# State tables of a convolution kernel: waves by chunk or by pairs of chunks

## The chip, the cores and the metric

The kernel runs on one core of one Trainium2 chip. The metric is the device time of one execution in microseconds (us), as a median over runs. The engines are TensorE (PE; its weight loads are PEld), VectorE (DVE), ScalarE (ACT), GpSimd (POOL) and SyncE (SP), which issues most DMAs. Each engine has its own in-order queue of instructions.

## The reference

The input u is 2048 x 512. After a layer norm over channels, two branches are computed and joined:

```
xn = layernorm(u)
K[d, l] = Re sum_n C[d,n] * dt[d] * B[d,n] * exp(dt[d] * A[d,n] * l)     # 512 channels, 128 states, 2048 steps
s = causal_convolution(xn, K) + xn * Dskip                               # by FFT in the reference
h = gelu(layernorm(xn) @ w1); shifted by -+1, -+2 steps per quarter of the channels; x1 = xn + hs @ w2
g = silu(x1 + gelu(layernorm(x1) @ w3) @ w4)                              # the MLP is 512 -> 1376 -> 512
out = u + s * g
```

A, B and C are complex. The kernel K of the convolution is a sum over 128 states of a decaying exponential times a wave, for each channel and step.

## The kernel before, in words

**The work.** The convolution goes through spectra: `u_stage1` and `u_spectra` transform the input, `kstage1` and `products(hf)` transform K and multiply, `inverse` and `finish` go back and add. The token mixing (`token_mixing`, with `h_pair` and `hs_pair`) and the MLP (`mlp`, eight groups of 256 steps) make the gate. The MLP runs in f16 pairs: `ph` by 12 matmuls of 256 columns, a gelu on ScalarE into `g`, two halves `ghl`, then 6 matmuls of 512 columns into `pa`.

**The state tables.** `tables(hf)` (lines 1060 to 1069) makes K for one half of the channels, in eight chunks of 32 channels (16 chunks in all, `CQ = 32`). It splits a step l into 64 fine positions and 32 coarse ones, so that K is a matrix product of a fine and a coarse table over the states. For a chunk `cc`:

- `phases` (line 989): two VectorE products of 128 x 1024 make the phases of the fine and the coarse table in `pt`; a shift by a large constant into `kt` rounds them to whole turns. The shift (`E.shift`) may run on ScalarE or VectorE.
- `remainders` (line 1011): one VectorE instruction of 128 x 2048 leaves the part of a turn.
- `waves` (line 1015): the absolute value into `kt` (`E.abs`, either engine), the sine of `pt` and the sine of `kt` plus a quarter turn (the cosine), both 128 x 2048 on ScalarE.
- `factors` and `sums` (lines 1021 and 1031): six VectorE products with the exponentials `mag`, `ea`, `eb`; then 256 small matmuls on TensorE, a copy `kev` and a DMA to HBM.

`block` (line 947), once for four chunks, makes those exponentials on ScalarE; `angle` (line 929), once for two chunks, small products. The pair `kt`, `pt` of a chunk lies in one of two buffers (`phpair`, line 779), taken in turn. In the trace all tiles of these two buffers have the name `pt`.

**Activation tables.** ScalarE holds one table set at a time. `TABLES` (line 104) gives the sets: exponentials are set 1, sine and silu set 2, gelu set 3. Before an operation of another set than the current one a table load is put in (line 512).

**The order of the work.** No engine's order is written by hand. All operations are recorded in a `Plan` (line 310) as objects with costs, and what they depend on is found from the places that they read and write. `order` (line 426) then runs through time: whenever an engine is free, it takes among its ready operations the one with the smallest due time, out of the list `DUE` (line 127, 1733 numbers, one for each operation in the order of recording), corrected by a few penalties: `SWITCH = 54.15` (line 258) where ScalarE would have to load another table, `KEEP` where TensorE would change its array mode, and `PREFER`, `AVOID`, `PREFERP`, `AVOIDP` where an operation may run on either of two engines:

```
if e == "ACT" and o.table and o.table != table:
    v += SWITCH
```

`together` (line 416) joins everything recorded inside it to one operation, which the planner places as one piece. It is used for the exponentials of a block and for groups of matmuls. While TensorE waits for longer, `issue` (line 506) fills its idle time with products of an identity.

Every instruction is issued in one of two lines, so the profile names line 515 for nearly all of them; 512 is the table load and 514 the filling products. The tiles tell them apart.

Of the kernel before, what the change touches and what calls it, by code (L numbers as in the profile page):

```python
# [27 lines left out]
TWO_PI = 6.283185  # L28
# [64 lines left out]
class Op:  # L93
# [163 lines left out]
)  # L257
SWITCH = 54.15
PREFERP, AVOIDP = 37.15, -7.22
PREFER, AVOID = -2.21, 23.48  # L260

# [404 lines left out]
def kernel(  # L666
# [393 lines left out]
    def tables(hf):  # L1060
        for cc in range(8 * hf, 8 * hf + 8):
            if cc * CQ % BQ == 0:
                block(cc * CQ // BQ)
# [464 lines left out]
```

## Time and profile before

| | |
|---|---|
| median of 3 runs | 564.96 us (564.07 to 565.45) |
| the profiled execution's own time | 567.52 us |
| its span, first to last instruction | 565.7 us |
| granted TensorE clock, mean | 0.986 |
| table loads on ScalarE | 49 of 1283 ns |

In a row of a group stand the engine, the operation, output and input tiles with partitions x elements, the count, then busy time, mean ns of one instruction, the idle time of the engine just before the group, and what ended it. In a row in order of time stand start, duration, engine, line and operation, in brackets an idle time before it and its releaser. Times in a row of windows are busy times inside that stretch.

### The profile page before, as it was taken

Reading aid. Unit: us, or ns where it says so; the run is one execution under the profiler, and the core shown is the slowest. Engines: PE = TensorE matmul, PEld = TensorE weight load, DVE = VectorE, ACT = ScalarE, POOL = GpSimd, SP = SyncE. Lnnn points to the kernel's source line nnn. Section 1 sums busy time; section 2 is a strip of 40 time slices with the busy share of each in tenths; the row PEclk is TensorE's granted clock in tenths of the full one; section 3 lists DMA queues with packets and bytes.
Section 4 is the critical chain, followed back from the end, with each engine's and each line's share of the span. In section 5 each row is a group of like instructions: output and inputs, shape, how many; then the busy total and the mean of one; then the engine's idle time right before and its main releaser. Section 6 shows DMA issues by size and latency. Waiting matters only on the chain.

```text
span 565.7 us, 14303 instructions
## 1 busy us (share of the span) xinstructions
PE 534.8 (95%) x6114; PEld 351.5 (62%) x6114; DVE 462.5 (82%) x706; ACT 411.6 (73%) x592; POOL 0.7 (0%) x6
## 2 busy tenths in 40 slices
PE   9979999999887899999999999999999999999982
PEld 8966776874443456567667666676665667567530
DVE  4999998999999989999999999999245257453566
ACT  2999997999968989978999997994436353232420
POOL 0000000000000000000000000000000000000000
PEclk9999999999999899999999999999999999999995
DMA  9996758345755224754224324326758558839977
GB/s 198 228 213 223 239 204 284 112 134 150 264 183 188 93 76 87 224 187 123 77 103 140 103 85 134 123 66 207 249 226 281 202 189 281 273 134 234 314 226 233
DMA packets 69695, 103.14 MB, mean 182 GB/s; under 512 B 14784, under 2 KB 48832, under 8 KB 68736
## 3 DMA queue, kind: packets, MB, share of 16 engines
q1 hardware_dynamic: 68864, 100.13, 57.5%
q10 hardware_dynamic: 768, 2.10, 1.1%
q8 instruction: 48, 0.79, 0.6%
q14 instruction: 15, 0.12, 0.1%
HBM read 64.46 MB, written 37.75 MB: 181 GB/s over the span
## 4 chain that ended last, share of the span: by engine, by line
PE 60%; DVE 20%; ACT 8%; DMA 7%; issue 3%; SPq 0%; DVEq 0%
PE pb L515 23%; PE pa L515 18%; DVE pt L515 11%; PE pc L515 10%; PE pd L515 9%; DVE X L515 4%; DMA X<-in_A_u_dram 4%; ACT pt L515 2%; ACT mag L515 2%; DVE pr L515 2%; ACT L512 1%; DMA rawA<-in_A_A_re_dram 1%; DMA cst<-c_gp 1%; DMA rawC<-in_A_C_im_dram 1%; DVE ghl L515 1%
## 5 line engine op out<-in xcount | busy, mean ns | idle before, releaser
L515 PE MATMUL pb<-x1T,w3h 128*128 128x256 f16 (+1 forms) x1056 | 123.2, 273 | 0.2 <-ACT g L515 0.2
L515 PE MATMUL pa<-w4h,ghl 128*128 128x512 f16 (+1 forms) x528 | 121.9, 379 | 0.0
L515 PEld LDWEIGHTS <-w3h 128*128 128x128 f16 (+1 forms) x1056 | 102.9, 100 | 23.7 <-issue 8.2
L515 PEld LDWEIGHTS <-ghl 128*128 128x128 f16 (+1 forms) x528 | 49.6, 98 | 61.7 <-issue 8.5
L512 ACT ACT_TABLE_LOAD x49 | 62.9, 1283 | 7.4 <-issue 5.9
L515 PE MATMUL pd<-w,hT 128*128 128x512 f32 x116 | 55.1, 617 | 6.4 <-DVE X L515 5.0
L515 PE MATMUL pb<-xT,w 128*128 128x256 f32 x256 | 59.4, 383 | 1.3 <-ACT xT L515 1.3
L515 DVE TENSOR_TENSOR pt<-mag,pt 128x1024 f32<-128x1024 f32 x48 | 57.6, 1215 | 0.7 <-ACT pt L515 0.7
L515 PEld LDWEIGHTS pb<-xT,w 128*128 128x128 f32 x256 | 47.2, 190 | 12.8 <-issue 3.2
L515 ACT ACTIVATE pt<-pt 128x2048 f32<-128x2048 f32 x28 | 53.3, 1907 | 0.3 <-DVE pt L515 0.2
L515 ACT ACTIVATE g<-pb,wsc 128x512 f32<-128x512 f32 (+1 forms) x48 | 30.8, 649 | 30.7 <-PE pb L515 28.6
L515 DVE SCALAR_TENSOR_TENSOR ghl<-g,wsc,ghl 128x512 f16<-128x512 f32 (+1 forms) x48 | 33.3, 700 | 22.4 <-ACT ghl L515 22.3
L515 ACT ACTIVATE ghl<-g,wsc 128x512 f16<-128x512 f32 (+1 forms) x37 | 24.7, 680 | 28.7 <-PE pa L515 28.5
L515 PEld LDWEIGHTS pd<-w,hT 128*128 128x128 f32 x116 | 21.9, 196 | 33.0 <-issue 25.9
L515 ACT ACTIVATE mag<-par 128x128 f32<-128x128 f32 x160 | 40.8, 460 | 0.5 <-DVE pt L515 0.4
L515 PE MATMUL pc<-pt 128*32 128x64 f32 x2048 | 34.3, 220 | 3.7 <-DVE pt L515 2.5
L515 PEld LDWEIGHTS pc<-pt 128*32 128x32 f32 x2048 | 30.0, 110 | 11.6 <-issue 7.4
L515 DVE TENSOR_TENSOR pt<-pt 128x2048 f32<-128x2048 f32 x16 | 36.5, 2281 | 0.2 <-ACT pt L515 0.2
L515 DVE SCALAR_TENSOR_TENSOR pt<-pt 128x2048 f32<-128x2048 f32 x16 | 36.2, 2279 | 0.0
L515 DVE TENSOR_TENSOR pr<-pd,uin 128x1024 f32<-128x1024 f32 x16 | 18.9, 1219 | 17.2 <-PE pd L515 17.2
L515 ACT ACTIVATE pt<-pt,halfpi 128x2048 f32<-128x2048 f32 x16 | 31.9, 1997 | 0.1
L515 DVE TENSOR_TENSOR pr<-pd,kh 128x1024 f32<-128x1024 f32 x16 | 19.3, 1220 | 11.6 <-PE pd L515 11.4
(149 smaller groups left out, 785.4 us busy)
## 6 DMA issues: line engine op xcount, KB each, us to landing
wst<-in_B_w_dram SPq DMA_DIRECT2D x20, 512.0 KB, 4.4
scr_Ud<-ue SPq DMA_DIRECT2D x16, 512.0 KB, 3.5
uin<-scr_Ud SPq DMA_DIRECT2D x32, 256.0 KB, 4.1
cst<-c_gp SPq DMA_DIRECT2D x16, 384.0 KB, 4.2
scr_Uh<-uh SPq DMA_DIRECT2D x8, 512.0 KB, 3.8
scr_Kfa<-k1e SPq DMA_DIRECT2D x8, 512.0 KB, 3.1
kin<-scr_Kfa SPq DMA_DIRECT2D x16, 256.0 KB, 3.9
scr_Zda<-z1e SPq DMA_DIRECT2D x8, 512.0 KB, 3.5
```

The costliest lines, as they stand in the source:

```text
L512: self.engines["ACT"].preload_act_table_set(SETS[table])
L515: ins = [getattr(self.engines[op.eng], name)(*args, **kw).ins for name, args, kw in op.calls]
```

## The change

`tables` takes two chunks at a time. The phases and remainders of both are recorded first, then the waves of both, then the factors and sums of each. `waves` gets both chunks; the absolute values remain operations of their own, and the four sine operations become one operation of the planner, which nothing else on ScalarE can enter:

```
-    def waves(cc):
-        kt, pt = heads[cc][4][:, 0], heads[cc][4][:, 1]
-        E.abs(kt[:, HALF:], pt[:, HALF:])
-        A.activation(pt[:, HALF:], pt[:, HALF:], AF.Sin, scale=-TWO_PI)
-        A.activation(kt[:, HALF:], kt[:, HALF:], AF.Sin, bias=halfpi[:, 0:1], scale=-TWO_PI)
+    def waves(ccs):
+        for cc in ccs:
+            kt, pt = heads[cc][4][:, 0], heads[cc][4][:, 1]
+            E.abs(kt[:, HALF:], pt[:, HALF:])
+        with plan.together(table=TABLES[AF.Sin]):
+            for cc in ccs:
+                kt, pt = heads[cc][4][:, 0], heads[cc][4][:, 1]
+                A.activation(pt[:, HALF:], pt[:, HALF:], AF.Sin, scale=-TWO_PI)
+                A.activation(kt[:, HALF:], kt[:, HALF:], AF.Sin, bias=halfpi[:, 0:1], scale=-TWO_PI)
...
     def tables(hf):
-        for cc in range(8 * hf, 8 * hf + 8):
-            if cc * CQ % BQ == 0:
-                block(cc * CQ // BQ)
-            if cc * CQ % AQ == 0:
-                angle(cc * CQ // AQ)
-            phases(cc)
-            remainders(cc)
-            waves(cc)
-            sums(cc, factors(cc))
+        for c2 in range(8 * hf, 8 * hf + 8, 2):
+            if c2 * CQ % BQ == 0:
+                block(c2 * CQ // BQ)
+            for cc in (c2, c2 + 1):
+                if cc * CQ % AQ == 0:
+                    angle(cc * CQ // AQ)
+                phases(cc)
+                remainders(cc)
+            waves((c2, c2 + 1))
+            for cc in (c2, c2 + 1):
+                sums(cc, factors(cc))
```

There are thus 24 operations fewer to plan, and the list `DUE` is another one, of 1709 numbers; all of it is replaced. So are the penalties:

```
-SWITCH = 54.15
-PREFERP, AVOIDP = 37.15, -7.22
-PREFER, AVOID = -2.21, 23.48
+SWITCH = 8.57
+PREFERP, AVOIDP = 0.93, 3.13
+PREFER, AVOID = 0.26, 2.43
```

The due times before spread wider (one in twenty lies below -314, one in twenty above 686) than those after (below -7 and above 494).

254 rows, old and new, of the table DUE are left out of this document.

## The prediction

> **What bounds the kernel now.** I read the page's shares and slices first, then a table by stage, then the groups on ScalarE and VectorE, and last the two engines in order of time around the table loads. The page:
>
> ```profile
> span 565.7 us, 14303 instructions
> PE 534.8 (95%) x6114; PEld 351.5 (62%) x6114; DVE 462.5 (82%) x706; ACT 411.6 (73%) x592; POOL 0.7 (0%) x6
> PE 60%; DVE 20%; ACT 8%; DMA 7%; issue 3%; SPq 0%; DVEq 0%
> ```
>
> TensorE is busy 95% of the span and carries 60% of the chain that ended last; ScalarE, whose work the change regroups, carries 8%. The average hides stages, so the windows come next (length, then busy time of PE, PEld, DVE, ACT and POOL, granted clock, DMA share, GB/s):
>
> ```profile
> 40.00:80.00 40.00, 39.52 (x190) 27.55 (x192) 39.72 (x101) 39.91 (x48) 0.00 (x0) 1.00 0.67 224
> 80.00:120.00 40.00, 38.60 (x569) 30.13 (x566) 37.41 (x39) 35.74 (x43) 0.00 (x0) 1.00 0.64 207
> 120.00:160.00 40.00, 37.90 (x439) 20.81 (x438) 39.76 (x62) 39.34 (x73) 0.00 (x0) 1.00 0.57 179
> 160.00:202.00 42.00, 34.41 (x439) 16.48 (x440) 40.43 (x46) 33.70 (x50) 0.00 (x0) 0.96 0.42 145
> 202.00:400.00 198.00, 197.59 (x2693) 132.10 (x2692) 192.86 (x266) 177.83 (x233) 0.00 (x0) 1.00 0.41 124
> 400.00:541.00 141.00, 140.54 (x1359) 88.08 (x1358) 64.52 (x79) 55.51 (x71) 0.00 (x0) 1.00 0.74 244
> 541.00:565.70 24.70, 11.51 (x179) 3.58 (x176) 16.96 (x19) 2.34 (x2) 0.00 (x0) 0.74 0.71 213
> ```
>
> From 202 to 541 us TensorE is idle for 0.41 + 0.46 = 0.87 us of 339. What lies there can be rearranged on ScalarE without moving the end, as long as TensorE stays fed. From 40 to 202 us TensorE is idle for 0.48 + 1.40 + 2.10 + 7.59 = 11.6 us, while VectorE is busy 157.3 of 162: there VectorE sets the pace. So two things decide: whether TensorE's stream after 202 gets holes, and whether the idle 11.6 us before it grow or shrink. The sine tables of chunks 0 to 7 lie in the first stretch, those of chunks 8 to 15 in the second.
>
> **The change, part by part.** No arithmetic is added or removed. What is regrouped, and its prices:
>
> ```profile
> L512 ACT ACT_TABLE_LOAD x49 | 62.9, 1283 | 7.4 <-issue 5.9
> L515 ACT ACTIVATE pt<-pt 128x2048 f32<-128x2048 f32 x28 | 53.3, 1907 | 0.3 <-DVE pt L515 0.2
> L515 ACT ACTIVATE pt<-pt,halfpi 128x2048 f32<-128x2048 f32 x16 | 31.9, 1997 | 0.1
> ```
>
> The second row mixes 16 sines with 12 absolute values (the other 4 are on VectorE); the third is the 16 cosines. One piece of four waves takes 2 x 1.91 + 2 x 2.00, less three overlaps of about 0.1, so 7.5 us.
>
> First saving: visits to the sine table. In ScalarE's order of time four loads lead to waves in the first half (67.63, 104.92, one at 137 and 155.36) and eight in the second, the first at 228.58 and the last at 372.18; the visit at 104.92 is shown whole:
>
> ```profile
> 67.63 1.28 ACT L512 ACT_TABLE_LOAD   x1
> 104.92 1.28 ACT L512 ACT_TABLE_LOAD   x1
> 106.22 2.00 ACT L515 ACTIVATE pt<-pt,halfpi 128x2048 f32<-128x2048 f32 x1
> 109.17 3.69 ACT L515 ACTIVATE pt<-pt 128x2048 f32<-128x2048 f32 x2
> 113.38 1.99 ACT L515 ACTIVATE pt<-pt,halfpi 128x2048 f32<-128x2048 f32 x1
> 115.39 1.28 ACT L512 ACT_TABLE_LOAD   x1
> 116.68 1.09 ACT L515 ACTIVATE hT<-pb 128x512 f32<-128x512 f32 x2
> 155.36 1.28 ACT L512 ACT_TABLE_LOAD   x1
> 228.58 1.28 ACT L512 ACT_TABLE_LOAD   x1
> 372.18 1.28 ACT L512 ACT_TABLE_LOAD   x1
> ```
>
> The visit at 104.92 already does all four waves of chunks 2 and 3, and the one at 67.63 those of chunks 0 and 1. Eight chunks in four visits is what pairs give, so the first half, where time is open, saves nothing. The second half goes from eight visits to four: up to eight loads fewer. A switch costs 1.28 for the load and about 0.12 for the overlap that two instructions without a load have (the two at 109.17 take 3.69 where twice 1.907 is 3.81), together 1.4; eight make 11.2 us of ScalarE's time, and the count falls from 49 towards 41. The other end is no fall: the planner's penalty for a switch drops from 54.15 to 8.57, so it may change tables more readily elsewhere. At the end this is worth 0 either way, as TensorE is full there.
>
> The Trainium skill ("ScalarE: Activation LUTs", What ACT_TABLE_LOAD costs) adds a drain of about 1380 ns to the 1283 ns of the load, about 2.66 us a switch. Here the hT activation at 116.68 starts within 0.01 us of the load's end, so the trace shows no such drain; by the page ScalarE would save 21 us, in the same place, and the sum would stand.
>
> Second: what pairs hold up. Both phase buffers belong to one pair until its sums, so while the four waves run VectorE has no table work except what follows the first sine and cosine. From 40 to 202 us the table tile takes 106.95 of VectorE's time, which leaves some 50 us of other work to set beside four pieces of 7.5 us plus a load each:
>
> ```profile
> 40.00:202.00 162.00, 106.95 (x76) 0.99 0.57 188
> 78.27 2.29 DVE L515 TENSOR_TENSOR pt<-pt 128x2048 f32<-128x2048 f32 x1 [0.21 <-ACT pt L515]
> 108.26 2.49 DVE L515 TENSOR_TENSOR pt<-mag,pt 128x1024 f32<-128x1024 f32 x2 [0.44 <-ACT pt L515]
> ```
>
> The two visits that are pairs already made VectorE wait 0.21 and 0.44 us: nothing new for chunks 0 to 3. Chunks 4 to 7 are not pairs now; their two pieces are new, in the stretch where TensorE is idle 2.10 and 7.59 us. The wait of each lies between nothing, or below, should the new order suit it (an earlier pair of phases costs no instruction), and load, sine and cosine uncovered, 1.28 + 1.91 + 2.00 = 5.2. I take a third of the upper end, 1.75 each, because the near rows speak for the low end but those pairs had the whole layer norm as cover. Behind a VectorE instruction that waits, in its queue, stand the additions to X of the token mixing, and TensorE waits for those, so this part reaches the end: 2 x 1.75 = +3.5. Moved up with the second chunk's phases go its shift and remainder (2.28 us on VectorE), on engines that must do them anyway; the four VectorE products that follow, the kev copy and its one store per chunk move later by the same order, and the SP queue is ordered anew by the same list.
>
> Third: gelus wait behind a piece. In the second half ScalarE is away from the MLP for load, piece and load, 10.1 us.
>
> ```profile
> 304.26 0.68 ACT L515 ACTIVATE g<-pb,wsc 128x512 f32<-128x512 f32 x1
> 314.00 0.69 ACT L515 ACTIVATE g<-pb,wsc 128x512 f32<-128x512 f32 x1
> 280.00:320.00 40.00, 39.91 (x611) 27.14 (x609) 39.85 (x47) 39.37 (x67) 0.00 (x0) 1.00 0.34 112
> 233.70 2.59 PE pa L515 x12
> 236.29 2.62 PE pb L515 x24
> ```
>
> It is away now from 304.26 to 314.00, 9.7 us, for 24 exponentials, and TensorE stays busy 39.91 of 40 us around it. The cover is the spectra and table matmuls put there. So 0. If that cover is gone, one round of MLP matmuls (2.59 + 2.62 = 5.2) is all that can run ahead, and each of four pieces shows 4.9.
>
> The Trainium skill ("Perfetto Trace Analysis", Optimizing Scalar/DVE Operations) says the opposite of the change: where ScalarE or VectorE are not saturated but cause bubbles on other engines, breaking up instructions lets work be completed sooner. From 160 to 202 us that is the case (ScalarE 33.70 of 42, TensorE with 7.59 idle), and a longer piece there goes against it; the 0.44 us above is all that an existing piece shows of it.
>
> Sum: 0 (loads) + 3.5 (two new pieces before 202 us) + 0 (four after). The profiled execution took 567.52, that is its span of 565.7 and 1.8 outside, 2.56 above the median of 564.96; 571.0 on it, so **568.5** on the median. Its own range is 566.7 to 572.
>
> **The rivals.** *Nothing shows* (chance 0.18): the handoffs stay covered as the two existing pairs are, waits of 0.2 to 0.4 us, and ScalarE's 11 us vanish beside a full TensorE: 565.0, anything within 563.3 to 566.7. The same time results if the change does not do what it says, because the planner's loads elsewhere come back under the lower penalty.
>
> *The freed ScalarE takes work from VectorE* (0.30), which ends faster. Eight absolute values and shifts sit on VectorE:
>
> ```profile
> L515 DVE TENSOR_SCALAR pt<-pt 128x2048 int32<-128x2048 int32 x4 | 4.9, 1216 | 0.0
> L515 DVE TENSOR_SCALAR pt<-pt 128x2048 f32<-128x2048 f32 x4 | 4.9, 1215 | 0.0
> ```
>
> Each costs ScalarE 1.9 to 2.0 instead of 1.22. With 11.2 us ScalarE takes about six, 7 us off VectorE. It decides only if the new order carries that relief back before 202 us, by moving some table work later; half of it arriving there gives 564.96 - 3.5 = 561.5, and all the idle 11.6 us bound it from below. For it: VectorE is full there, and every due time is new. Against it: the loads fall after 202 us.
>
> *The MLP starves* (0.14): two of the four pieces uncovered, 9.8 us, 574.8; all four 584.6. It decides as soon as an MLP piece of TensorE has no spectrum or table matmul to stand beside the wave piece. For it: the four waves can no longer be broken up by a gelu. Against: the 9.7 us gap shown.
>
> **How the numbers follow.** My forecast of a small loss has 0.38, the starving 0.14: slower by over 0.3% (1.7 us, about what a measurement of this kernel can tell from no change) 0.52. Same has 0.18 and faster 0.30. The range runs from 559.5, past the faster rival's 561.5, to 576, past two starved pieces; it leaves out the idle time's full bound and three or four starved pieces. The whole list of due times is replaced, so terms of a few us of either sign from the new order alone are within it.
>
> **What would show it.** Right: about 41 to 45 table loads; four visits of four adjacent waves in each half; TensorE idle from 120 to the start of its full stream by some 3 to 4 us more, with VectorE waiting on ScalarE's pt there; after that no more than 1 us idle up to the last MLP matmul. Wrong: TensorE's full stream starting earlier than 202 us by more than 2 us (the faster rival), holes of several us beside wave pieces later, released by g or ghl (the starving), or more than 49 loads. It would also be wrong if the tail after the last MLP matmul, 24.7 us now, changes by over 2 us, for which nothing in the rows above speaks.

## The result, and the profile after

The changed kernel takes 573.56 us (median of 4 runs, 570.26 to 574.41), the kernel before 564.52 beside it (4 runs, 563.48 to 565.45): ratio 1.0145, 95% interval 1.0112 to 1.0177, so 9.0 us slower. The forecast was 568.5, 3.5 us slower, with a range from 559.5 to 576. The direction was right, the size was not, and the place was not either. (One execution below, the profiled one of after_chain_first, was disturbed at 3073.55 us; its trace is not read and its median leaves it out.)

The page of the changed kernel, and its windows by stage (columns as before: length, busy time of PE, PEld, DVE, ACT and POOL, granted clock, DMA share, GB/s):

```profile
span 571.8 us, 14339 instructions
PE 540.2 (94%) x6136; PEld 353.9 (62%) x6136; DVE 472.9 (83%) x713; ACT 404.7 (71%) x583; POOL 0.7 (0%) x6
PE 60%; DVE 7%; issue 1%; DMA 1%; DVEq 0%
```

```profile
40.00:80.00 40.00, 39.92 (x195) 28.08 (x192) 40.00 (x82) 39.48 (x49) 0.00 (x0) 1.00 0.66 222
80.00:120.00 40.00, 38.59 (x438) 28.40 (x438) 34.73 (x57) 34.34 (x39) 0.00 (x0) 1.00 0.66 212
120.00:160.00 40.00, 35.04 (x484) 19.59 (x483) 38.64 (x47) 36.87 (x64) 0.00 (x0) 0.91 0.55 182
160.00:202.00 42.00, 38.54 (x414) 19.92 (x413) 41.80 (x56) 36.24 (x45) 0.00 (x0) 0.96 0.34 115
202.00:400.00 198.00, 194.93 (x2717) 129.65 (x2716) 196.68 (x262) 171.65 (x243) 0.00 (x0) 1.00 0.39 121
400.00:541.00 141.00, 140.33 (x1389) 89.47 (x1387) 67.59 (x86) 54.80 (x68) 0.00 (x0) 1.00 0.75 243
541.00:571.80 30.80, 17.70 (x247) 6.05 (x245) 20.83 (x25) 3.57 (x4) 0.00 (x0) 0.78 0.71 216
```

TensorE's busy time is not all work: the planner puts filler products on the identity where it expects a wait. They have a line of their own, 514 in the kernel before and 510 in the changed one (groups by line):

```profile
L514 PE MATMUL pd<-ident 128*128 128x128 f32 x134 | 15.3, 275 | 0.0
L514 PE MATMUL pc<-ident 128*128 128x128 f32 x14 | 1.7, 275 | 0.0
```

```profile
L510 PE MATMUL pd<-ident 128*128 128x128 f32 x154 | 17.6, 276 | 1.1 <-ACT z1e L511 1.1
L510 PE MATMUL pa<-ident 128*128 128x128 f32 x12 | 1.5, 275 | 0.0
L510 PE MATMUL pc<-ident 128*128 128x128 f32 x4 | 0.6, 275 | 0.0
```

So the 6.1 us of span come apart in three: idle time 565.7 - 534.8 = 30.9 before and 571.8 - 540.2 = 31.6 after, +0.7; filler 17.0 and 19.7, +2.7; the same other products 534.8 - 17.0 = 517.8 and 540.2 - 19.7 = 520.5, +2.7, most of which goes with a lower clock (0.91 at 120 to 160 us, where it was 1.00): 116 products of the token mixing take 1.9 us more, in the first two rows below.

The times of the two profiled executions are 567.52 and 573.65. The medians lie 2.9 us further apart, because the profiled execution of before was 3.0 above its median. A second pair of traces lies closer to the medians: both kernels without the table loads for the exponentials, the first experiment, which changed neither time by more than 1.3 us. Their spans are 563.6 and 571.7 us. Of these 8.1 us, +0.4 are idle time (30.8 and 31.2), +2.7 filler (17.0 and 19.7 again) and +5.0 the other products (515.8 and 520.8); the same 116 products account for 4.0 of the last. In each pair the kernel before comes first:

```profile
L515 PE MATMUL pd<-w,hT 128*128 128x512 f32 x116 | 55.1, 617 | 6.4 <-DVE X L515 5.0
L511 PE MATMUL pd<-w,hT 128*128 128x512 f32 x116 | 57.0, 637 | 4.7 <-DVE X L511 4.7
L517 PE MATMUL pd<-w,hT 128*128 128x512 f32 x116 | 53.4, 601 | 6.2 <-DVE X L517 4.7
L513 PE MATMUL pd<-w,hT 128*128 128x512 f32 x116 | 57.4, 641 | 5.7 <-DVE X L513 5.7
```

So slower products cost 2.7 to 5.0 us, by the execution of before that one compares with.

By stage, idle and filler together (stage length, less PE's busy time, plus the filler in it) were 13.5 us from 40 to 202 us and 0.4 from 202 to 400 before; they are 9.9 and 5.8 now. The loss of waiting and filling lies after 202 us, and 4.6 of it in one place. It is steady: three other traces of each kernel in its own order (without the exponentials' loads, without the sines' loads, with short remainders) have 0.1 to 0.4 us there for the kernel before and 5.8 to 6.0 for the changed one. TensorE in order of time there, in the changed kernel (start, duration, in brackets what it waited for), with the copy and the load that belong to it:

```profile
302.82 2.00 PE L511 MATMUL pd<-pr,cst 64*128 64x256 f32 x16
304.86 0.34 SPq L511 DMA_DIRECT2D cst<-c_gp  x1
304.87 1.01 ACT L511 COPY z1e<-pd 128x1024 f32<-128x1024 f32 x1 [1.35 <-PE pd L511]
305.93 2.72 PE L510 MATMUL pd<-ident 128*128 128x128 f32 x22 [1.11 <-ACT z1e L511]
309.42 1.10 PE L511 MATMUL pd<-kin,cst 64*32 64x256 f32 x32 [0.77 <-DMA cst<-c_gp]
```

The same step of the convolution before:

```profile
298.40 2.00 PE L515 MATMUL pd<-pr,cst 64*128 64x256 f32 x16
300.33 2.79 PE L515 MATMUL pb<-x1T,w3h 128*128 128x256 f16 x24
300.44 0.35 SPq L515 DMA_DIRECT2D cst<-c_gp  x1
302.96 0.60 PE L515 MATMUL pb<-ident,x1n 128*128 128x128 f32 x4
303.39 1.46 PE L515 MATMUL pa<-w4h,ghl 128*128 128x512 f16 x6
304.94 1.10 PE L515 MATMUL pd<-kin,cst 64*32 64x256 f32 x32
```

The last product with pr frees the table cst; the next one is loaded (304.86 to 309.42, 4.6 us from the issue to the product that needs it), the result is copied, and only then can the next block's spectrum begin. Before, three pieces of the MLP stand in that gap, 304.94 - 300.4 = 4.5 us of work. In the changed kernel nothing does: 22 filler products and 1.9 us of idle time. VectorE and ScalarE are both at work meanwhile; TensorE waits first for the copy z1e and last for the reload. VectorE has a part in what could have stood there: the MLP's next two operations `ghl` run on it only at 306.61 and 308.55, behind two products of the state tables (303.00 to 305.35) and an addition to X.

### The profile page after: what moved, and what is told of

It reads as the page before. It is cut to its first block, busy times and chain, and to the rows that moved or that the text cites. A ratio compares the mean times of both kernels' runs of the same rounds, so it can differ in the third digit from the quotient of the medians.

```text
span 571.8 us, 14339 instructions
## 1 busy us (share of the span) xinstructions
PE 540.2 (94%) x6136; PEld 353.9 (62%) x6136; DVE 472.9 (83%) x713; ACT 404.7 (71%) x583; POOL 0.7 (0%) x6
## 4 chain that ended last, share of the span: by engine, by line
PE 60%; DVE 7%; issue 1%; DMA 1%; DVEq 0%
PE pb L511 21%; PE pa L511 19%; PE pd L511 12%; PE pc L511 8%; DVE X L511 3%; DVE pt L511 3%; DMA cst<-c_gp 1%; DVE ghl L511 0%; DVE w3h L511 0%; DVE x1T L511 0%; DVE k1e L511 0%; DVE pab L511 0%; DVE w4h L511 0%; DVE EB L511 0%; DVE x1n L511 0%
## 5 line engine op out<-in xcount | busy, mean ns | idle before, releaser
L511 PE MATMUL pd<-w,hT 128*128 128x512 f32 x116 | 57.0, 637 | 4.7 <-DVE X L511 4.7
L511 ACT ACTIVATE pt<-pt 128x2048 f32<-128x2048 f32 x30 | 57.0, 1906 | 1.5 <-DVE pt L511 1.4
L511 ACT ACTIVATE g<-pb,wsc 128x512 f32<-128x512 f32 (+1 forms) x48 | 30.5, 648 | 35.8 <-PE pb L511 30.9
L511 PE MATMUL pc<-pt 128*32 128x64 f32 x2048 | 33.1, 220 | 2.4 <-issue 1.6
L511 ACT ACTIVATE pt<-pt,magic 128x2048 f32<-128x2048 f32 x13 | 26.0, 1997 | 5.9 <-DVE pt L511 5.8
L511 DVE TENSOR_TENSOR pr<-pd,uin 128x1024 f32<-128x1024 f32 x16 | 18.9, 1217 | 12.1 <-PE pd L511 12.0
```

Source lines behind the costliest of these rows:

```text
L511: ins = [getattr(self.engines[op.eng], name)(*args, **kw).ins for name, args, kw in op.calls]
```

## The experiments

All times are medians; ratios are to runs of the kernel before beside them on the same chip. "Own order" means that the planner's order of all instructions is kept, and only what the edit names differs.

### Is it ScalarE: visits and table loads?

In both kernels, in their own orders, the exponentials of mag and EB (first pair of runs) or the 32 sines and cosines (second pair) become plain identity, for which no table has to be loaded.

```
+            if op.eng == "ACT" and op.table and plain(op):
+                op.calls = [(name, args[:2] + (AF.Identity,), kw) for name, args, kw in op.calls]
-            if op.eng == "ACT" and op.table and op.table != table:
+            elif op.eng == "ACT" and op.table and op.table != table:
```

> Kernel before in its own order of instructions, with the 208 exponentials of the blocks (tiles mag and EB) replaced by a plain scaling of the same size, which needs no table: 41 table loads instead of 49. The exponentials are left out of the result. Theory A (what costs the time is where the pairs put VectorE's table work in front of the additions to X; table loads are hidden): within 2 us of the kernel before, 562.5 to 566.5. Theory B (what costs is that ScalarE changes tables more often for the exponentials, 10 visits instead of 7, because the penalty for a switch is lower): 0 to 3 us faster, as this kernel has the fewer of these visits.

> Kernel after in its own order, the same replacement: 33 table loads instead of 47. The exponentials are left out of the result. Theory A: 571.5 to 575, no more is gained than in the kernel before. Theory B: at least 5 us faster than the kernel after, 568.5 or less, since 14 loads or 18 us of ScalarE's time go.

> Kernel before in its own order, with the 32 sines of the state tables replaced by a plain scaling of the same size, which needs no table: 30 loads instead of 49. The sines are left out of the result. My prediction's term (the loads of the second half are hidden beside a full TensorE): 563 to 566. If table loads for the waves are worth something: 558 or less, since 19 loads are 24 us of ScalarE's time.

> Kernel after in its own order, the same replacement: 34 loads instead of 47. The sines are left out of the result. Theory A: 571 to 575. Theory B: also small, 570 to 575, as the visits for the waves are not the ones it blames.

Measured: without exponential visits 564.90 (0.9992, 0.9956 to 1.0027) and 572.31 (1.0136, 1.0080 to 1.0193), with 41 and 33 loads left; without the sines' loads 563.14 (0.9970, 0.9942 to 0.9998) and 572.05 (1.0133, 1.0076 to 1.0190), with 30 and 34. The page without the sines' loads, of the kernel before and of the changed one:

```profile
PE 533.8 (95%) x6114; PEld 350.5 (63%) x6114; DVE 462.1 (82%) x706; ACT 387.2 (69%) x573; POOL 0.7 (0%) x6
```

```profile
PE 539.9 (95%) x6136; PEld 354.4 (62%) x6136; DVE 472.9 (83%) x713; ACT 388.0 (68%) x570; POOL 0.7 (0%) x6
```

Before, 19 loads and 24 us of ScalarE's time gave 1.7 us, in the changed kernel 13 loads and 17 us gave 1.5, and the difference between the kernels stayed at 8.9 (7.4 without the exponentials' loads). Neither the saving that the change aims at nor the visits that came back elsewhere reach the end with more than these 1.5 to 1.7 us. The theory that more exponential visits cost the time fell: it asked for 568.5 or less.

### Is it VectorE: the additions behind a pair's work?

In the changed kernel the first addition into X, whose product is there at about 122 us, runs at 139.68, behind the sums of one pair and the phases of the next. TensorE stands idle for 1.99 us before 138.38 and for 1.71 before 140.94, and only the second wait is released by that addition. The edit moves each such addition up to where its product is ready:

```
+    for op in [o for o in order if o.eng == "DVE" and o.calls[0][0] == "tensor_add" and o.calls[0][1][0].tensor.name.startswith("X")]:
+        at = {o.idx: k for k, o in enumerate(order)}
+        k = max([at[d] for d in op.deps] + [j for j, o in enumerate(order) if o.start < op.ready]) + 1
+        if k < at[op.idx]:
+            order.remove(op)
+            order.insert(k, op)
```

> The changed kernel with each of the additions into X that VectorE ran later than its product was there moved up in VectorE's queue, ahead of the phases and sums of the pairs (the first by some 17 us, four others by one to four instructions). Theory A (the additions behind a pair's work starve TensorE): the hole at 136 to 140 us and the half clock behind it go, 2.7 to 5 us less, 568 to 571 us. Theory C (VectorE's total up to 400 us sets the end): the hole goes, but VectorE has as much to do, idle or filler comes back at 202 to 400 us, and the time is within 1.5 us of the changed kernel's, 572 to 575 us.

Measured: 575.04 (1.0182, 1.0149 to 1.0215), so no gain. VectorE and then TensorE in order of time, in this run:

```profile
121.52 1.22 DVE L511 TENSOR_TENSOR X<-X,pd 128x1024 f32<-128x1024 f32 x1 [0.90 <-PE pd L511]
```

```profile
142.45 1.10 PE L511 MATMUL pa<-uin,cst 64*32 64x256 f32 x32 [1.55 <-ACT uh L511]
150.58 1.96 PE L511 MATMUL pa<-uin,cst 64*32 64x256 f32 x32 [3.40 <-DVE uh L511]
```

The addition ran at 121.52, VectorE itself waited 0.90 for it, and TensorE's wait moved on to the copy uh, which was now late in its turn. Of the clock's loss some came back (the 116 products take 55.0 us after 57.0), but TensorE's idle time rose from 31.6 to 34.4. So moving the additions alone gains nothing, and the theory that their place in the queue makes the 9 us fell; what their place costs in an order that suits it, this run cannot price.

The next three runs move copies out of PSUM between the engines, because VectorE has 10.4 us more to do in the changed kernel (472.9 after 462.5), 16 of its copies being ue, uh and xT where there were 6:

```
+        if op.eng == "DVE" and op.psum and "ACT" in op.alts and name in ("ue", "uh", "xT"):
+            op.eng, op.calls = "ACT", op.alts["ACT"][1]
```

> The changed kernel in its own order, but for the 16 evacuations of the input's spectra and transposes (ue 8, uh 3, xT 5, each 1.22 us on VectorE), which ScalarE now runs at the same places of the order. Theory C (the cost is the work that the new list of due times put on VectorE, which is 99% busy from 202 to 400 us): VectorE loses 19.5 us before 202 us, its table work gets through earlier, the 5.8 us of idle and filler products at 202 to 400 us shrink by 3 us or more, and the time is 564 to 569 us. Theory A (the cost is the pairing itself, VectorE's two chunks of phases and sums ahead of the additions): within 2 us of the changed kernel's, 571 to 575 us, with the hole at 136 to 140 us still there. Against both: ScalarE, given 19 us, holds up the spectra, and the time is over 576 us.

> As the run with the spectra's and transposes' evacuations on ScalarE, and the evacuations ahead of 420 us into k1e, kh, z1e and kev too (some 11 more). Theory C: VectorE is below 96% from 202 to 400 us and the time is another 0 to 3 us lower than there, 562 to 568 us. Theory A: 571 to 575 us. If ScalarE now becomes the later one in the second half (it was 87% busy there, and 11 copies are 14 us more), the holes come back behind ACT's copies and the time is over 575 us.

> The kernel before in its own order, with 10 evacuations (ue 5, uh 3, xT 2) moved from ScalarE to VectorE, about what the changed kernel's planner moved. Theory C: VectorE gets 12 us more ahead of 202 us, where it was 93 to 99% busy, is late for the rest, and the time rises by 3 to 9 us, to 568 to 574. Theory A: no pair has been made, so under 2 us, 564 to 567.

Measured: 597.19 (1.0569), 615.29 (1.0900) and 576.36 (1.0206, 1.0172 to 1.0240). The first of them from 40 to 80 us:

```profile
40.00:80.00 40.00, 31.03 (x147) 21.95 (x147) 29.25 (x66) 39.50 (x47) 0.00 (x0) 0.92 0.46 150
```

In the changed kernel both engines were full there (40.00 and 39.48 of 40). With the copies on ScalarE, VectorE falls to 29.25, waiting with TensorE for ScalarE. Moved either way a copy comes late in a queue that was laid out without it, so these runs price a disturbed order, and say of the changed kernel's own split only that it isn't one that can be shifted by hand. All three lie outside what the two theories forecast; the first two are what was set down against both.

A cleaner question is to relieve VectorE of the same work in both kernels and leave every queue as it is. The 16 remainders are cut short:

```
+        if kw.get("op1") == ALU.subtract and args[2] == MAGIC:
+            op.calls = [(name, (args[0][:, :64], args[1][:, :64], MAGIC, args[3][:, :64]), kw)]
```

> The changed kernel in its own order with 16 instructions of VectorE cut short: each chunk's remainder is taken over 64 of its 2048 columns (the rest keep the phase as it was), so that VectorE has 16 x 2.2 = 35 us less to do and every queue its order. Theory V (the 9 us are VectorE's lateness: its queue is full from 40 to 400 us, and the products wait behind it): the holes shrink in both kernels, and the changed one comes to within 4 us of the other one so cut (2.7 us of its filler products stay in TensorE's queue in any case). Theory O (the order itself, who is placed before whom, with transfers and ScalarE's copies in between): both fall by about as much and the difference stays at 7 to 10 us.

> The kernel before in its own order with the same 16 instructions cut short. Its TensorE has 0.4 us of idle and filler at 202 to 400 us, so what it gains it gains ahead of 202: 2 to 8 us, 557 to 563 us. Theory V: it gains 5 us or more less than the changed kernel does. Theory O: as much as that.

Measured: 569.02 (1.0090, 1.0061 to 1.0120) and 562.47 (0.9979, 0.9951 to 1.0007). 31 us less work on VectorE gave 4.5 and 2.1 us; the difference went from 9.0 to 6.6, which the intervals do not tell from no change. It lies between the two theories, within 4 us (V) and 7 to 10 (O). The changed kernel, the window and then TensorE at the hole:

```profile
202.00:400.00 198.00, 194.86 (x2717) 129.22 (x2710) 181.36 (x266) 171.96 (x242) 0.00 (x0) 1.00 0.41 126
```

```profile
298.50 2.00 PE L511 MATMUL pd<-pr,cst 64*128 64x256 f32 x16
301.61 2.72 PE L510 MATMUL pd<-ident 128*128 128x128 f32 x22 [1.11 <-ACT z1e L511]
304.50 1.10 PE L511 MATMUL pd<-kin,cst 64*32 64x256 f32 x32 [0.17 <-DMA cst<-c_gp]
```

VectorE is down from 196.68 to 181.36 us in this stage, yet idle and filler of TensorE are 5.9 us as before, and the hole (300.5 to 304.5) is there with the same wait for z1e. So with the order kept, less work on VectorE does not close that hole. Whether the planner would have put MLP pieces there if VectorE had had less to do, this run does not show, as TensorE's queue was the same by design.

### Is it the order: a reload with nothing behind it?

The chain at 300 us (products with pr, copy z1e, the loads of cst and uin, the store) was moved in both kernels. In the one before it goes behind the three MLP pieces that covered it and six more products; in the changed one ahead of two groups of table products and four transposes, and its 22 filler products are left out.

```
+    chain = [o for o in order if o.idx in (951, 952, 953, 954, 955, 956)]
+    order = [o for o in order if o not in chain]
+    k = [o.idx for o in order].index(1219) + 1
+    return order[:k] + chain + order[k:]
```

> The kernel before with the mirrored edit: the same chain (its products with pr at 298.4 us, the copy and the loads) goes behind 24 + 24 products of the MLP, four transposes and six more products (4.9 us), so that nothing is left between the reload and the product that needs it. Theory O: a hole of 4 to 4.6 us opens, as in the changed kernel, nothing gives it back, and the time rises by 3 to 5 us, to 567.5 to 569.5. If it is hidden later: under 1.5 us, 564 to 566.

> The changed kernel in its own order but for one place: at 300 us the convolution's last products with pr (16, 2.0 us), the copy of their result (z1e) and the loads that they release (cst, uin) go ahead of two groups of table products (2.0 us) and four transposes (0.7 us), and the 22 filler products behind them are left out. Theory O (the hole of 4.6 us there is the chain product, copy and reload with nothing behind it in TensorE's queue): the hole shrinks to 2 to 3 us, and the time falls by 1.5 to 2.6 us, to 571 to 572. Theory V (VectorE is what TensorE waits for there): the hole moves on to the next products and the time stays, 573 to 575 us.

Measured: before_chain_last 570.75 (1.0115, 1.0082 to 1.0149), 6.7 us slower than 564.09. TensorE in order of time:

```profile
301.14 1.04 PE L515 MATMUL pa<-w4h,ghl 128*128 128x512 f16 x4 [0.89 <-DVE ghl L515]
302.11 2.00 PE L515 MATMUL pd<-pr,cst 64*128 64x256 f32 x16
308.01 1.96 PE L515 MATMUL pd<-kin,cst 64*32 64x256 f32 x32 [3.91 <-DMA cst<-c_gp]
309.91 2.00 PE L515 MATMUL pa<-w4h,ghl 128*128 128x512 f16 x6
```

One displaced chain of six operations opens a hole of 3.91 us, with 0.89 in front of it, and the products behind it run slower: 1.96 instead of 1.10 and 2.00 instead of 1.47, 1.4 us more. Together 6.2 of the 6.7 (4.6 to 8.4 by the interval). Nothing later gave it back: idle and filler from 202 to 400 us are 5.9 us, and none from 400 to 541. So the kernel before, given a reload with nothing behind it, loses the reload's whole length and more.

after_chain_first took 573.40 (1.0156, 1.0130 to 1.0183), the changed kernel's time; 1.5 to 2.6 us less were expected, so this was a miss. Whether the hole only moved on, or whether its shorter rest, now without filler, cost the clock as it did above, can't be said without a trace of it. That the hole in the changed kernel can be given back is therefore not shown.

### Is it the pieces, or the list that orders everything else?

The change replaces two things at once: pieces of four waves, and all due times and constants. These runs part them. The lists of due times were found by search, each starting from the order of one kernel or the other; PAIRS names the pairs (by their first chunk) that are pieces, and all other waves are free.

```
-        with plan.together(table=TABLES[AF.Sin]):
+        with plan.together(table=TABLES[AF.Sin]) if ccs[0] in PAIRS else nullcontext():
```

four_pairs has PAIRS = 0, 10, 12, 14, five_pairs also 8, seven_pairs also 4 and 6, and eight_pairs all; after_list_chunks_free is the code of before with a list that was searched on from the changed kernel's order; before_other_list is the code of before with another list searched on from its own.

> The pieces of four waves undone: the code of the kernel before, whose planner may place each wave of each chunk by itself, with a list of due times that was searched on from the changed kernel's order (chunks kept near where the changed kernel has them, constants searched as well). Theory L (the new list puts the rest of the work, copies, additions and gelus, in a worse order, whatever the waves do): undoing the pieces brings back little, 569 to 575 us. Theory G (the grouping costs: two chunks at a time make VectorE's phases, remainders and sums late or early as a block): with the pieces free the search gets most of it back, 563 to 568 us.

> Pieces of four waves for the first pair of the first half and the last three of the second, the other four pairs free, with a list that was searched on from the order of the kernel before, adding one pair at a time. Theory L: the pieces cost little in a list of their own, 562 to 567 us. Theory G: half of the 9 us for half of the pieces, 568 to 571 us.

> As four_pairs, and the first pair of the second half too, so that all of the second half goes by pieces (four visits for eight chunks) and the three later pairs of the first half are free. Theory L: as four_pairs within 3 us, 562 to 569 us. Theory G: more than half of the 9 us, 569 to 573 us. If the second half alone holds the cost (it is there that the changed kernel has 5.8 us of idle and filler products), the time is that of the changed kernel, 571 to 575 us, and four_pairs lies between.

> The kernel before, every wave free, with another list of due times and constants, searched on from its own. It shows how far a list alone moves the time. Theory L: lists differ by several us whatever is grouped; this one should be 1 to 4 us below the kernel before, 560.5 to 563.5 us. Theory G says nothing of it; if it is over 566 us, an order that should be no worse is, and comparisons between searched lists tell no less than 3 us.

> As five_pairs, and the third and the fourth pair of the first half as pieces too; only the second pair of the first half is free. Theory L (list): within 3 us of five_pairs, 566 to 572 us. Theory G (the grouping, in the first half): 571 to 577 us.

> All eight pieces, the changed kernel's code, with a list searched on from the order of the kernel before, pair by pair. Theory L: 566 to 572 us, below the changed kernel's 573.6. Theory G: at least the changed kernel's, 573 to 580 us, whatever the list; then the step from seven to eight pairs is the price of the second pair of the first half.

Measured, with TensorE's idle and filler time of the stages worked out as above:

| kernel | pieces | time, us | ratio, interval | 40 to 202 us | 202 to 400 us |
|---|---|---|---|---|---|
| before | 0 | 564.5 | 1 | 13.5 | 0.4 |
| before_other_list | 0 | 564.06 | 1.0012, 0.9984 to 1.0039 | 14.6 | 0.2 |
| after_list_chunks_free | 0 | 577.27 | 1.0204, 1.0166 to 1.0242 | 14.1 | 5.7 |
| four_pairs | 4 | 571.49 | 1.0103, 1.0071 to 1.0135 | 11.2 | 3.3 |
| five_pairs | 5 | 568.72 | 1.0065, 1.0040 to 1.0091 | 12.1 | 5.2 |
| seven_pairs | 7 | 581.52 | 1.0307, 1.0269 to 1.0345 | 15.5 | 6.4 |
| eight_pairs | 8 | 577.86 | 1.0234, 1.0203 to 1.0265 | 16.6 | 3.8 |
| after | 8 | 573.56 | 1.0145, 1.0112 to 1.0177 | 9.9 | 5.8 |

Against what was expected: four_pairs and eight_pairs lie on the side of the theory that the grouping costs (G), five_pairs on that of the list (L); seven_pairs and after_list_chunks_free are slower than both had them, and before_other_list, with times from 563.3 to 568.8, is not the 1 to 4 us faster that L hoped for.

First, the hole does not need the pieces. With every wave free again (in the second half one chunk's waves run at 282.10 and 283.92, the next one's at 302.70 and 305.39) but a list from the changed kernel's order, TensorE still runs into it:

```profile
308.70 2.00 PE L522 MATMUL pd<-pr,cst 64*128 64x256 f32 x16
310.63 0.66 PE L522 MATMUL pb<-ident,x1n 128*128 128x128 f32 x4
311.81 2.72 PE L521 MATMUL pd<-ident 128*128 128x128 f32 x22 [0.53 <-ACT z1e L522]
314.79 1.10 PE L522 MATMUL pd<-kin,cst 64*32 64x256 f32 x32 [0.26 <-DMA cst<-c_gp]
```

Nor do the pieces need the hole. In eight_pairs, all eight pieces but a list from the order of before, MLP products again fill the time ahead of the product that needs the reloaded table, and TensorE waits nowhere from 202 to 400 us for z1e or cst:

```profile
300.37 4.05 PE L524 MATMUL pa<-w4h,ghl 128*128 128x512 f16 x18
304.35 1.09 PE L524 MATMUL pd<-kin,cst 64*32 64x256 f32 x32
```

So this hole follows the list and not the pieces. That list was searched for a kernel with pieces, though, and eight_pairs pays in other places (16.6 us of idle and filler from 40 to 202 us), so this does not say that pieces are free.

Second, the pieces of the second half need not make holes beside them. In five_pairs all four are there, and from 240 us on:

```profile
240.00:400.00 160.00, 159.98 (x2139) 108.02 (x2139) 152.63 (x196) 133.81 (x175) 0.00 (x0) 1.00 0.34 111
```

Its loss in this stage lies from 202 to 240 us, and nearly all of it ahead of the first of these pieces, which starts at 236.27. The whole price of five pieces, list included, is 565.04 x 0.0065 = 3.7 us (2.3 to 5.1). Third, the later pairs of the first half stay open. All lists that have them as pieces are slow, 573.6 to 581.5, which speaks for a price of the grouping there; but after_list_chunks_free is as slow without a piece, seven_pairs is slower than eight_pairs, and four_pairs than five_pairs. A searched list is thus good to some 3 to 4 us only, and a better one for eight pieces may exist.

## Why the prediction was right in sign and wrong in size

- *Table loads, worth 0 at the end*: right, and shown to within 1.7 us by the runs without them. The count fell to 47 and not to 41 to 45. The second half has its four visits and 22 loads from 202 to 410 us where there were 28, but between 40 and 202 us there are 14 instead of 10, as the other end of that term allowed. That the lower penalty did it is not shown.

- *Two new pieces make VectorE wait, 2 x 1.75 = +3.5*: wrong. VectorE's waits for the waves from 40 to 202 us, before and then after:

```profile
DVE pt L515 <- ACT pt L515: 0.9, 3, 0.4
```

```profile
DVE pt L511 <- ACT pt L511: 0.2, 1, 0.2
```

They fell from 0.9 to 0.2 us in all. The additions did come late behind a pair's work, but moving them up gained nothing. Idle and filler went down, from 9.7 to 8.4 us between 120 and 202 us, where 3 to 4 more were forecast, and from 13.5 to 9.9 between 40 and 202. The forecast's whole 3.5 came from this term, so that its sign was right is luck: the loss was put where waiting fell, and nothing where it rose. The remark on breaking up instructions, set against the change there, speaks of something that it does not do: a sine still takes 1.91 us and a cosine 1.99, and only their order changed. Nor was it ScalarE that TensorE mostly waited for from 160 to 202 us: VectorE released 5.0 of the 7.6 us.

- *Third term, "The cover is the spectra and table matmuls put there. So 0."*: this is the step that failed. From 202 to 400 us TensorE lost 5.4 us more than before, and the sign set down for it, no more than 1 us idle up to the last MLP product, failed with 3.07 + 0.67 = 3.7 us to 541, filler not counted. The term looked for waits of the MLP beside the pieces, covered by the spectra. What came was the reverse: the spectra's own chain (product, copy, reload) lost the MLP pieces that had covered it, at 304.8 us, some 15 us after the piece that ended at 289.6. That a cover would be lost was put in the rival "the MLP starves", with 0.14. The price named there, 4.9 us, lies close to the 4.6 found by chance only: it was ScalarE's absence less one round of MLP products, and what came is the length of a copy and a reload. The rival's sign "released by g or ghl" was wrong, the release being z1e and cst.

- *Slower products*, 2.7 us between the two profiled executions and 5.0 in the other pair of traces: no term of the sum held them. Where they can be placed, they stand behind waits before 202 us: 8 products at 140.94 take 5.96 us where their like take 3.70, and 16 at 186.02 take 8.83 where they take 7.13 (last section).

- *What the change is*: the prediction said that the new list alone may move a few us either way and left it to the range. With the pieces undone the hole stays, and with eight pieces on another list it is gone, so the list should have been a rival with a price of its own. The rival in which freed ScalarE takes work off VectorE failed: VectorE got 10.4 us more.

- *Tail*, forecast unchanged: right. From the last MLP product to the end it is 20.1 us before and 20.0 after (the 24.7 named there counts from 541 us, while the last MLP product ends at 545.63).

What stays open: between the two profiled executions, 5.4 us of idle and filler after 202 us and 2.7 of slower products, against a gain of 2.0 in the idle and filler time of the other stages, make the 6.1 of the spans. In the other pair of traces 5.4, 5.0 and a gain of 2.3 make 8.1 of the 9.0. How much of it the pieces, those of the first half above all, force on any list is not settled, and no edit of the changed kernel gave its hole back.

## What to carry to other kernels

With TensorE full, 17 to 24 us saved on ScalarE were worth 1.7 us at most here, and the regrouping cost what the new order did to TensorE's queue. So look for each chain of product, copy and reload, and name what stands in TensorE's queue between its ends. A change that comes with a new order of everything is two changes; try the new order without the regrouping, and the regrouping with another order, before crediting or blaming either.

## What the hardware showed beyond that

A short idle time can cost the clock too. In the changed kernel, windows and then products of TensorE, and in the last row a product group of the kernel before:

```profile
140.00:143.50 3.50, 2.56 (x3) 1.17 (x4) 3.27 (x3) 3.50 (x4) 0.00 (x0) 0.50 0.63 192
186.00:190.00 4.00, 3.98 (x6) 1.68 (x7) 4.00 (x10) 3.97 (x4) 0.00 (x0) 0.57 0.01 4
```

```profile
140.94 5.96 PE L511 MATMUL pd<-w,hT 128*128 128x512 f32 x8 [1.71 <-DVE X L511]
186.02 8.83 PE L511 MATMUL pd<-w,hT 128*128 128x512 f32 x16 [2.25 <-DVE X L511]
162.73 7.13 PE L511 MATMUL pd<-w,hT 128*128 128x512 f32 x16 [0.48 <-DVE X L511]
182.12 7.13 PE L515 MATMUL pd<-w,hT 128*128 128x512 f32 x16 [2.18 <-DVE X L515]
```

A wait of 2.25 us at 183.8 was followed by a granted clock of 0.57, and 16 products took 8.83 us where they take 7.13 behind a wait of 0.48. The Trainium skill ("TensorE: Matmul & The Clock Gate", What's actually happening) has the clock fall after an idle window of about 3.4 us; here 2.25 us were enough once. They are not always: in the kernel before, a wait of 2.18 us left the same 16 products at 7.13. The hole at 304.8, as long as 4.6 us but with 22 filler products in it, kept the products behind it at full speed (1.10 us for 32, as before), where the unfilled 3.91 us of before_chain_last made them take 1.96. So the filler does its work; it cannot give the time back.
